# Attention rows scaled by VectorE out of PSUM, and a list schedule that counts the shared SBUF port

## The chip, the core and the metric

The kernel runs on one core of a Trainium2 chip, as one program. Its time is the device time of one execution in microseconds (us). The names of the engines are those of the profile: PE is TensorE's matmul and PEld its weight load, DVE is VectorE, ACT is ScalarE, POOL is GpSimd, SP issues the transfers. PSUM is the memory that PE writes its results to, SBUF the one that the other operands lie in.

## The reference

Three layers follow one another: a causal attention with a decay, and two MLPs. The sizes are batch 4, 8 heads, 576 positions, head size 64; then 2304 tokens of width 512, with hidden widths 1536 and 2048.

```python
def _attn_ref(q, k, v, f):
    scores = scale * np.matmul(q, k.transpose(0, 1, 3, 2))
    cum = np.cumsum(np.log(np.clip(f, 0.0001, 1.0)), axis=-1)
    decay = cum[:, :, :, None] - cum[:, :, None, :]
    scores = np.where(causal, -1000000000.0, scores + decay)
    scores = scores - np.max(scores, axis=-1, keepdims=True)
    attn = np.exp(scores)
    attn = attn / (np.sum(attn, axis=-1, keepdims=True) + 1e-09)
    return np.matmul(attn, v)

def _moe_ref(x, w_a, w_b, w_out):
    return ((x @ w_a) * (x @ w_b)) @ w_out

def _moe2_ref(x, w_in, w_out):
    h = x @ w_in
    g = np.where(h >= 1, h, np.where(h <= -1, 0.0, (h + 1) ** 2 / 4))
    return g @ w_out
```

The attention's result, with the heads side by side, is the first MLP's input, and the MLPs' matmuls are the bulk of the arithmetic.

## The kernel before

Two parts follow one another. The early part holds all the attention and, beside it, the first group of the first MLP for three of the four batches; the late part holds the rest of the MLPs.

**Attention.** Heads go in pairs (`pp`), 16 in all, four to a batch. A head has five chunks of 128 query rows; the fifth has 64 real rows, so the two heads of a pair share one. A pair is seven rounds (`PAIR_ROUNDS`): chunks 0 and 1, then 2, then 3 of the first head, the shared fifth chunk, then the same three of the second head. A round makes scores in a PSUM tile `s` (PE), adds the mask and finds each row's extreme `nm` (DVE, tile `prob`; the order lists this instruction as ISA), takes the exponential (ACT), transposes blocks of `prob` into a PSUM tile `tp` (PE), splits them into two fp16 parts, `th` (ACT) and `tl` (DVE), and multiplies them with the values, also two parts, `vh` and `vl`, into the PSUM tile `o` (PE). The values carry one more column of ones, so column 64 of `o` is the row's sum. The tile `o` has one PSUM bank in all; it is filled 48 times, three times per pair: first head, fifth chunk, second head.

**The scaling of the rows** (end of `pv_step`) is what the change is about. Before, ACT copies `o` into SBUF (`on`, `on4`); DVE makes the divisor `z` from column 64 and `sc`, takes its reciprocal, and the rows are multiplied into `xt`: by GpSimd for a head's four full chunks (128x256), by two DVE instructions (64x64 each) for the fifth chunk.

**Scaling the values.** For each pair, `v_max`, `v_top`, `v_scale` and `v_split` find a power of two per head and split the values. `v_top` ends with `dg`, a 2x2 DVE instruction that PE waits for.

**The order.** In the early part no call issues an instruction at once. An object, `Plan`, records them all and then writes a list schedule: `cost` gives each operation a duration, `forward` steps through time engine by engine and takes, of the operations that are ready, the one of the highest rank, `backward` makes new ranks from the last round's finish times, and after 20 rounds the best order found is issued. Where the model sees PE idle for over `HEAT` = 150 ns, `forward` puts filler matmuls (`mm<-mask`, 128x224, results unused) into PE's queue. Each engine then works through its queue in order, and waits where an operand isn't there. In the trace, all that `Plan` issues has line L279 (L298 after the change); the fillers are L932 (L948). The late part is not recorded by `Plan`; its first matmuls have the lines L512 to L514 (`mm3`).

**Weights.** Blocks of weights come as 64-bit numbers (`wraw`) and are decoded by ACT (`wm`, `wr`), DVE (`wm` clamped, `wt`) and GpSimd (`wt`, `whi`, `wlo`); a few of these blocks are decoded in the early part.

Of the kernel before, what the change touches and what calls it, by code (L numbers as in the profile page):

```python
# [21 lines left out]
P = 128  # L22
# [17 lines left out]
NPB = 3  # L40
LAND = 1030.0
SWITCH = 300.0
HEAT = 150.0
COLD = 6000.0
NEVER = 1.0e18
# [24 lines left out]
class Plan:  # L70
# [5 lines left out]

    def __init__(self, nc):
        self.nc = nc
        self.ops = []
        self.seen = {}  # L80
        self.boost = 0.0
        self.heat = None
# [29 lines left out]
    @staticmethod  # L112
    def cost(engine, method, out, src, args):
        n = max(x.size() // x.shape[0] for x in [out] + (src if engine == "vector" else []))
        if engine == "tensor":
            if method == "transpose":
                return 109.0, 53.0
            size = mybir.dt.size(args["rhs"].dtype)
            passes = 4 if args["rhs"].dtype == F32 else 1
            return passes * max(n / 2.4, 24.0) + 3.0, (107.0 if size == 4 else 27.0)  # L120
        if engine == "vector":
            fast = method in ("tensor_scalar", "tensor_copy", "memset")
            fixed = 66.0 + 61.0 * any(x.shape[-1] == 1 for x in src)
            return fixed + (0.53 if fast else 1.05) * n, 0.0
        if engine == "scalar":
            near = any(x.space == bass.MemoryType.PSUM for x in src)
            return (187.0 if "bias" in args or "scale" in args and not near else 51.0 if near else 90.0) + 0.833 * n, 0.0
        if engine == "gpsimd":
            if method == "tensor_tensor":
                return 55.0 + 2.26 * n, 0.0  # L130
            return 76.0 + 115.0 * any(x.shape[-1] == 1 for x in src) + n, 0.0
        return (650.0 if out.shape[0] == 64 else 475.0), 0.0

    def add(self, engine, method, a, kw):
        names = {"out": a[0]} if a else {}
        names.update(kw)
        out = names["out"]
        writes = [out] + [x for x in (kw.get("accum_out"),) if x is not None]
        reads = [x for x in list(a[1:]) + [x for k, x in kw.items() if k not in ("out", "accum_out")]
                 if isinstance(x, bass.AP)]  # L140
        if method == "tensor_tensor_reduce":
            writes.append(reads.pop())
        me, need = len(self.ops), set()
        for ap, wr in [(x, False) for x in reads] + [(x, True) for x in writes]:
            if ap.space == bass.MemoryType.DRAM:
                if ap.tensor.name not in self.nc_inputs:
                    box = (0, 1, 0, 1, False)
                else:
                    continue
            else:  # L150
                box = Plan.area(ap)
            psum = ap.space == bass.MemoryType.PSUM
            if psum:
                box = (box[0], box[1], 0, 2048, box[4] and box[3] - box[2] == 2048)
            stores, loads = self.seen.setdefault(ap.tensor.name, ([], []))
            need.update(j for old, j, _ in stores if Plan.meet(old, box))
            if wr or psum:
                need.update(j for old, j, other in loads if Plan.meet(old, box) and (wr or other != engine))
            if wr:
                stores[:] = [x for x in stores if not Plan.within(x[0], box)]  # L160
                loads[:] = [x for x in loads if not Plan.within(x[0], box)]
            (stores if wr else loads).append((box, me, engine))
        need.discard(me)
        dur, load = Plan.cost(engine, method, out, reads, names)
        done = dur
        if engine == "sync":
            done = (1275.0 if out.shape[0] == 64 else 625.0, out.size() * mybir.dt.size(out.dtype) / 360.0)
        self.ops.append((engine, method, a, kw, sorted(need), dur, load, done, self.boost))

    def lag(self, j, i):  # L170
        a, b = self.ops[j], self.ops[i]
# [17 lines left out]
    def forward(self, rank):  # L189

        ops, n = self.ops, len(self.ops)
        missing = [len(op[4]) for op in ops]
        ready = [0.0] * n
        wait = {e: [] for e in Plan.ENGINES}
        for i, op in enumerate(ops):
            if not missing[i]:
                wait[op[0]].append(i)
        soon = {e: min((ready[i] for i in wait[e]), default=NEVER) for e in Plan.ENGINES}
        free = {e: 0.0 for e in Plan.ENGINES}
        last = {e: 1e9 for e in Plan.ENGINES}  # L200
        begin, finish, fill = [0.0] * n, [0.0] * n, []
        moved = 0.0
        for _ in range(n):
            t, e = min((max(free[e], soon[e]), e) for e in Plan.ENGINES)
            idle = t - free[e]
            i, best = -1, 0.0
            for j in wait[e]:
                if ready[j] <= t:
                    value = rank[j] - SWITCH * max(0.0, ops[j][6] - last[e] - idle)
                    if i < 0 or value > best or value == best and j < i:  # L210
                        i, best = j, value
            wait[e].remove(i)
            _, _, _, _, _, dur, load, done, _ = ops[i]
            t = max(t, free[e] + load - last[e])
            if e == "sync":
                moved = max(t + done[0], moved) + done[1]
                done = moved + LAND - t
            if e == "tensor" and t - free[e] >= HEAT:
                step = 100.0 if free[e] > COLD else 190.0
                fill += [(free[e] + j * step, n) for j in range(int((t - free[e] - HEAT) // step) + 1)]  # L220
            begin[i], finish[i] = t, t + done
            free[e], last[e] = t + dur, dur
            for j, gap in self.after[i]:
                ready[j] = max(ready[j], t + done + gap)
                missing[j] -= 1
                if not missing[j]:
                    wait[ops[j][0]].append(j)
                    soon[ops[j][0]] = min(soon[ops[j][0]], ready[j])
            soon[e] = min((ready[j] for j in wait[e]), default=NEVER)
        return begin, finish, fill  # L230
# [42 lines left out]
    def issue(self):  # L273
        for i in self.order():
            if i == len(self.ops):
                self.heat()
                continue
            engine, method, a, kw = self.ops[i][:4]
            getattr(getattr(self.nc, engine), method)(*a, **kw)  # L279
        self.ops, self.seen = [], {}  # L280


class Ring:
# [16 lines left out]
def tile_decay_attention__then__moe__then__moe2(  # L300
# [417 lines left out]
    def v_top(pp):  # L718
# [5 lines left out]
        nc.vector.tensor_scalar(m2[:, 0:1], m2[:, 0:1], 2.0 ** -86, None, ALU.max)  # L724
        nc.vector.tensor_scalar(m2i[:, 0:1], m2i[:, 0:1], 0x7F800000, None, ALU.bitwise_and)
        dg = sm_p.tile([2, 2], BF16, name="dg", tag="dg")
        nc.vector.tensor_scalar(dg, ident[0:2, 0:2], m2[:, 0:1], 2.0 ** -14, ALU.mult, ALU.mult)
        vst[pp] = dg

    def v_scale(pp):  # L730
# [101 lines left out]
    def pv_step(k):  # L832
# [5 lines left out]
        if a is not None:  # L838
# [5 lines left out]
            for c in chunks:  # L844
                pv(o[:, c, :], pv_seq(where, c, a, slice(0, P), vv))
            if chunks[-1] == NCH - 2:
                on = sm_p.tile([P, NCH - 1, D + 1], F32, name="on", tag="on", bufs=1)
                nc.scalar.copy(on, o)
                z = sm_p.tile([P, NCH - 1], F32, name="z", tag="z")
                nc.vector.tensor_scalar(z, on[:, :, D], PSC * 1e-9, sc[:, a:a + 1], ALU.add, ALU.mult)  # L850
                nc.vector.reciprocal(z, z)
                nc.gpsimd.tensor_tensor(xt[:, 0:NCH - 1, h * D:(h + 1) * D], on[:, :, 0:D],
                                        z.unsqueeze(2).to_broadcast([P, NCH - 1, D]), ALU.mult)
        else:
            o = ps_o.tile([P, 512], F32, name="o", tag="o")[:, 0:D + 1]
            on = sm_p.tile([P, D + 1], F32, name="on4", tag="on4", bufs=1)
            z = sm_p.tile([P, 1], F32, name="z4", tag="z4")
            halves = [slice(i * TAIL, (i + 1) * TAIL) for i in range(2)]
            seqs = [pv_seq(where, NCH - 1, i, halves[i], vv) for i in range(2)]
            for j in range(len(seqs[0])):  # L860
                for i in range(2):
                    l, r = seqs[i][j]
                    nc.tensor.matmul(o[halves[i], 0:r.shape[1]], lhsT=l, rhs=r, start=j == 0,
                                     stop=j == len(seqs[0]) - 1)
            nc.scalar.copy(on, o)
            for i in range(2):
                rows = slice(i * TAIL, (i + 1) * TAIL)
                nc.vector.tensor_scalar(z[rows], on[rows, D:D + 1], PSC * 1e-9, sc[rows, i:i + 1], ALU.add, ALU.mult)
            nc.vector.reciprocal(z, z)
            for i in range(2):  # L870
                rows = slice(i * TAIL, (i + 1) * TAIL)
                h = (2 * pp + i) % H
                nc.vector.tensor_scalar(xt[rows, NCH - 1, h * D:(h + 1) * D], on[rows, 0:D], z[rows], None, ALU.mult)

    NHH = B * H

# [191 lines left out]
```

## Time and profile before

| | |
|---|---|
| median of 3 runs (least to most) | 1097.97 us (1097.09 to 1098.0) |
| the profiled execution | 1095.04 us |
| its span, first to last instruction | 1093.2 us |
| PE busy | 1060.0 us (97%) |
| DVE busy | 663.5 us (61%) |
| ACT busy | 482.7 us (44%) |
| POOL busy | 605.6 us (55%) |
| last early (L279) instruction on POOL ends | 285.4 us |

The trace is of one execution. Busy is the time in which an engine had at least one instruction running; a DVE instruction's profiled span includes the time for which it is held after it was issued, and it overlaps a little with the next one's. Matmuls are pipelined, so the span of one is longer than the step to the next. The chain of waits goes back from the end of a stretch: at each step to what released the instruction, or to the one before it on its engine. A share of busy time over the whole span mixes the early and the late part, which have different limits, so the rows below are by stretches.

### The profile page before, as it was taken

The numbers are of one execution on the slowest core, as the hardware profiler recorded it, in microseconds if no ns is written. First come the engines' busy times: TensorE is split into PE (matmuls) and PEld (weight loads), VectorE is DVE, ScalarE is ACT, GpSimd is POOL, SyncE is SP. The second block draws the span as 40 slices with busy tenths as digits, with TensorE's granted clock in tenths as the row PEclk, the third lists the DMA queues.
The fourth block names the chain that finished last, engine by engine and source line by source line (L and its number), as shares of the span: only waits on it lengthen the run. The fifth ranks groups of instructions, "written<-read, shape, count | busy, mean of one in ns | idle before, by whom it ended". The sixth has DMA issues, their size and how long they took to land.

```text
span 1093.2 us, 19541 instructions
## 1 busy us (share of the span) xinstructions
PE 1060.0 (97%) x7475; PEld 1000.9 (92%) x7475; DVE 663.5 (61%) x1388; ACT 482.7 (44%) x970; POOL 605.6 (55%) x594
## 2 busy tenths in 40 slices
PE   7898889999899999999999999999999999999998
PEld 5677788998899999999999999999999999999998
DVE  6999989878873462552742833832684487355333
ACT  5788768877541231221321333643552234233221
POOL 7688778665692461641722856932772296156121
PEclk7999989999999999999999999999999999999999
DMA  8444534421230120110210300210220021010111
GB/s 243 144 143 123 164 108 139 128 83 50 62 113 20 38 79 1 59 58 1 77 39 1 98 19 1 78 39 1 78 78 1 1 97 58 1 40 10 57 46 64
DMA packets 22830, 72.12 MB, mean 66 GB/s; under 512 B 2840, under 2 KB 5912, under 8 KB 22736
## 3 DMA queue, kind: packets, MB, share of 16 engines
q1 hardware_dynamic: 22736, 70.87, 21.1%
q8 instruction: 59, 0.97, 0.4%
q14 instruction: 35, 0.29, 0.1%
HBM read 60.26 MB, written 5.96 MB: 61 GB/s over the span
## 4 chain that ended last, share of the span: by engine, by line
PE 76%; DVE 12%; POOL 5%; DMA 3%; issue 2%; ACT 1%; DVEq 0%; SPq 0%; POOLq 0%; ACTq 0%
PE mm L513 21%; PE mm L512 21%; PE mm L514 21%; PE s L279 4%; PE mm L279 4%; PE tp L279 4%; PE o L279 2%; DVE prob L279 2%; DVE tl L279 2%; POOL wlo L479 2%; DMA wraw<-in_w_dram 2%; DVE z L279 1%; POOL wt L466 1%; DVE wt L463 1%; DVE wm L457 1%
## 5 line engine op out<-in xcount | busy, mean ns | idle before, releaser
L513 PE MATMUL mm<-xl,whi 128*128 128x432 f32 (+1 forms) x896 | 299.7, 335 | 1.6 <-DVE xl L926 1.6
L514 PE MATMUL mm<-xh,wlo 128*128 128x432 f32 (+1 forms) x896 | 299.5, 335 | 0.0
L512 PE MATMUL mm<-xh,whi 128*128 128x432 f32 (+1 forms) x896 | 298.8, 335 | 0.1
L513 PE MATMUL mm<-al,whi 128*128 128x432 f32 (+1 forms) x640 | 212.6, 336 | 0.1
L514 PE MATMUL mm<-ah,wlo 128*128 128x432 f32 (+1 forms) x640 | 211.9, 335 | 0.0
L512 PE MATMUL mm<-ah,whi 128*128 128x432 f32 (+1 forms) x640 | 201.9, 336 | 2.2 <-ACT ah L567 2.2
L626 POOL TENSOR_TENSOR al<-tmp,ah 128x432 fp32r<-128x432 f32 (+1 forms) x96 | 103.8, 1082 | 169.2 <-ACT ah L625 169.2
L513 PEld LDWEIGHTS mm<-xl,whi 128*128 128x128 f32 x896 | 168.2, 188 | 5.8 <-DVE xl L926 1.9
L514 PEld LDWEIGHTS mm<-xh,wlo 128*128 128x128 f32 x896 | 168.2, 188 | 3.9
L512 PEld LDWEIGHTS mm<-xh,whi 128*128 128x128 f32 x896 | 167.8, 188 | 4.3 <-DVE tmp L566 0.4
L568 POOL TENSOR_TENSOR al<-tmp,ah 128x432 fp32r<-128x432 f32 (+1 forms) x64 | 67.9, 1062 | 175.4 <-ACT ah L567 175.4
L512 PEld LDWEIGHTS mm<-ah,whi 128*128 128x128 f32 x640 | 118.0, 188 | 6.9 <-ACT ah L567 3.6
L513 PEld LDWEIGHTS mm<-al,whi 128*128 128x128 f32 x640 | 119.9, 188 | 4.6 <-POOL al L568 1.5
L514 PEld LDWEIGHTS mm<-ah,wlo 128*128 128x128 f32 x640 | 119.8, 188 | 3.4
L623 ACT ACTIVATE tmp<-tmp,half 128x432 f32<-128x432 f32 (+1 forms) x96 | 59.1, 616 | 133.3 <-DVE tmp L622 132.9
L566 DVE TENSOR_TENSOR tmp<-mm,tmp 128x432 f32<-128x432 f32 (+1 forms) x64 | 35.0, 548 | 135.1 <-PE mm L514 135.0
L466 POOL TENSOR_TENSOR wt<-wt,wr 128x512 int32<-128x512 int32 x60 | 82.3, 1371 | 15.4 <-DVE wt L463 14.7
L279 ACT ACTIVATE prob<-prob,nm 128x128 f32<-128x128 f32 (+3 forms) x144 | 81.1, 584 | 20.4 <-DVE nm L279 19.3
L479 POOL TENSOR_TENSOR wlo<-wt,whi 128x512 fp32r<-128x512 f32 x62 | 88.4, 1427 | 2.4
L624 DVE TENSOR_TENSOR tmp<-tmp,mm 128x432 f32<-128x432 f32 (+1 forms) x96 | 52.9, 552 | 58.4 <-ACT tmp L623 55.7
L622 DVE TENSOR_SCALAR tmp<-mm 128x432 f32<-128x432 f32 (+1 forms) x96 | 53.2, 554 | 56.6 <-PE mm L514 56.3
L279 PE MATMUL tp<-ident,prob 128*128 128x128 f32 x400 | 78.1, 290 | 6.0 <-DVE m L279 3.5
(127 smaller groups left out, 1999.1 us busy)
## 6 DMA issues: line engine op xcount, KB each, us to landing
wraw<-in_w_dram SPq DMA_DIRECT2D x68, 512.0 KB
raw<-in_qk_dram SPq DMA_DIRECT2D x26, 608.0 KB
vraw<-in_v_dram SPq DMA_DIRECT2D x16, 320.0 KB
qk<-q SPq DMA_DIRECT2D x28, 160.0 KB
out_dram<-tmp SPq DMA_DIRECT2D x16, 216.0 KB
cum_d<-xh SPq DMA_DIRECT2D x1, 1216.0 KB
y<-in_qk_dram SPq DMA_DIRECT2D x2, 608.0 KB
out_dram<-tmp SPq DMA_DIRECT2D x8, 144.0 KB
```

The costliest lines, as they stand in the source:

```text
L279: getattr(getattr(self.nc, engine), method)(*a, **kw)
L466: nc.gpsimd.tensor_tensor(t, t, r, ALU.add)
L479: nc.gpsimd.tensor_tensor(lo, t.rearrange("p (u c) -> p u c", u=UB), V(hi), ALU.subtract)
L512: nc.tensor.matmul(o, lhsT=wh, rhs=xh, start=first, stop=False)
L513: nc.tensor.matmul(o, lhsT=wh, rhs=xl, start=False, stop=False)
L514: nc.tensor.matmul(o, lhsT=wl, rhs=xh, start=False, stop=last)
L566: after(4, lambda: nc.vector.tensor_tensor(pr, ob, asb, ALU.mult))
L568: after(6, lambda: nc.gpsimd.tensor_tensor(al, pr, V(ah), ALU.subtract))
L622: nc.vector.tensor_scalar(t, o, 1.0, -1.0, ALU.min, ALU.max)
L623: after(1, lambda: nc.scalar.activation(t, t, AF.Square, scale=0.5, bias=half))
L624: after(2, lambda: nc.vector.tensor_tensor(r, t, o, ALU.max))
L626: after(4, lambda: nc.gpsimd.tensor_tensor(al, r, V(ah), ALU.subtract))
```

## The change

Two things change. First, the scaling of the rows reads `o` in PSUM: ACT's copies are gone, `z` is made from `o`, and all the products into `xt` are DVE's; `dg` is written by two instructions of one column each. Second, `Plan` knows which operations use the SBUF port that DVE shares with GpSimd (`shares`): in `forward` such an operation starts only after the other engine's last such one has ended, and one that would be held loses rank (`PORT` = 10 per ns). Two durations in `cost` are raised as well. The late part's code is the same.

```diff
             passes = 4 if args["rhs"].dtype == F32 else 1
-            return passes * max(n / 2.4, 24.0) + 3.0, (107.0 if size == 4 else 27.0)
+            return passes * max(n / 2.4, 24.0) + (14.0 if size == 4 else 3.0), (107.0 if size == 4 else 27.0)
...
             if method == "tensor_tensor":
-                return 55.0 + 2.26 * n, 0.0
+                return 95.0 + 2.26 * n, 0.0
...
+    def shares(engine, method, out, src):
+        if engine == "gpsimd":
+            return True
+        if engine != "vector" or out.space == bass.MemoryType.PSUM:
+            return False
+        wide = [x for x in src if x.space != bass.MemoryType.PSUM and x.size() // x.shape[0] > 1]
+        if any(x.space == bass.MemoryType.PSUM for x in src):
+            return False
+        return len(wide) > 1 or len(wide) == 1 and method in ("tensor_scalar", "tensor_copy")
...
+            held = max(0.0, port["vector" if e == "gpsimd" else "gpsimd"] - t)
...
-                    value = rank[j] - SWITCH * max(0.0, ops[j][6] - last[e] - idle)
+                    value = rank[j] - SWITCH * max(0.0, ops[j][6] - last[e] - idle) - PORT * held * self.port[j]
...
+            if self.port[i]:
+                t += held
+                port[e] = t + dur
...
-        nc.vector.tensor_scalar(dg, ident[0:2, 0:2], m2[:, 0:1], 2.0 ** -14, ALU.mult, ALU.mult)
+        for i in range(2):
+            nc.vector.tensor_scalar(dg[:, i:i + 1], ident[0:2, i:i + 1], m2[:, 0:1], 2.0 ** -14, ALU.mult, ALU.mult)
...
-                on = sm_p.tile([P, NCH - 1, D + 1], F32, name="on", tag="on", bufs=1)
-                nc.scalar.copy(on, o)
                 z = sm_p.tile([P, NCH - 1], F32, name="z", tag="z")
-                nc.vector.tensor_scalar(z, on[:, :, D], PSC * 1e-9, sc[:, a:a + 1], ALU.add, ALU.mult)
+                nc.vector.tensor_scalar(z, o[:, :, D], PSC * 1e-9, sc[:, a:a + 1], ALU.add, ALU.mult)
                 nc.vector.reciprocal(z, z)
-                nc.gpsimd.tensor_tensor(xt[:, 0:NCH - 1, h * D:(h + 1) * D], on[:, :, 0:D],
+                nc.vector.tensor_tensor(xt[:, 0:NCH - 1, h * D:(h + 1) * D], o[:, :, 0:D],
                                         z.unsqueeze(2).to_broadcast([P, NCH - 1, D]), ALU.mult)
...
-            nc.scalar.copy(on, o)
...
-                nc.vector.tensor_scalar(z[rows], on[rows, D:D + 1], PSC * 1e-9, sc[rows, i:i + 1], ALU.add, ALU.mult)
+                nc.vector.tensor_scalar(z[rows], o[rows, D:D + 1], PSC * 1e-9, sc[rows, i:i + 1], ALU.add, ALU.mult)
...
-                nc.vector.tensor_scalar(xt[rows, NCH - 1, h * D:(h + 1) * D], on[rows, 0:D], z[rows], None, ALU.mult)
+                nc.vector.tensor_scalar(xt[rows, NCH - 1, h * D:(h + 1) * D], o[rows, 0:D], z[rows], None, ALU.mult)
```

The whole early order is written anew. At DVE, for the last head of the first batch, stood before (`z4` and `on4` are the fifth chunk's, `s` and `tp` are PSUM tiles; the number behind a name is its buffer):

```order
L279 TENSOR_SCALAR xt_128<-on4_0_165,z4_1_173 64x64
L279 ISA prob1_122,nm_3_157<-s_2_152,mask_104 128x320
L279 ISA nm_3_157 128x1
L279 TENSOR_SCALAR z_1_168<-on_0_161,sc_0_142 128x4
L279 SCALAR_TENSOR_TENSOR tl_0_150<-tp_1_141,th_0_149 128x384
L279 RECIPROCAL z_1_168<-z_1_168 128x4
L279 TENSOR_SCALAR xt_128<-on4_0_165,z4_1_173 64x64
L279 SCALAR_TENSOR_TENSOR tl_2_159<-tp_0_138,th_2_158 128x384
```

And on the same engine at the same head stands now:

```order
L298 ISA prob0_121,nm_2_151<-s_1_147,mask_104 128x512
L298 ISA nm_2_151 128x1
L298 TENSOR_SCALAR z_1_166<-o_0_155,sc_0_142 128x4
L298 TENSOR_SCALAR wt_0_169<-wm_0_168 128x512
L298 RECIPROCAL z_1_166<-z_1_166 128x4
L298 SCALAR_TENSOR_TENSOR tl_0_150<-tp_1_141,th_0_149 128x384
L298 TENSOR_TENSOR xt_128<-o_0_155,z_1_166 128x4x64
L298 SCALAR_TENSOR_TENSOR tl_2_159<-tp_0_138,th_2_158 128x384
```

The product into `xt` has come to DVE from GpSimd, two places behind the reciprocal, and `o` is read from the first to the last of these steps; a weight step `wt` and a `tl` stand between them.

On PE, between the second head of the third pair and the first head of the fourth, stood before (`o` is the bank with the results, `tp` the transposes, `s` the scores):

```order
L279 MATMUL o_0_155<-vh0_124,tl_2_159 128x65
L279 MATMUL tp_0_138<-ident_103,prob1_122 128x128 x3
L279 MATMUL s_0_144<-k1_1_116,q1_1_115 128x384
L279 MATMUL tp_1_141<-ident_103,prob2_123 128x128 x3
L279 MATMUL s_0_144<-qk2_1_117 128x384
L279 MATMUL tp_1_141<-ident_103,prob2_123 128x128
L279 LDWEIGHTS th_0_149
L279 MATMUL o_0_155<-vh1_125,th_0_149 128x65
```

And on PE at the same place stands now:

```order
L298 MATMUL o_0_155<-vh0_124,tl_2_159 128x65
L298 MATMUL tp_1_141<-ident_103,prob2_123 128x128 x4
L298 MATMUL s_0_144<-k1_1_116,q1_1_115 128x384
L298 MATMUL s_0_144<-qk2_1_117 128x384
L298 MATMUL s_1_147<-k1_1_116,q1_1_115 128x512
L298 MATMUL s_1_147<-qk2_1_117 128x512
L298 MATMUL tp_2_148<-ident_103,prob0_121 128x128 x3
L298 MATMUL tp_0_138<-ident_103,prob0_121 128x128 x2
L298 MATMUL s_2_152<-k1_0_113,q1_0_112 128x128
L298 MATMUL s_2_152<-qk2_0_114 128x128
L298 LDWEIGHTS th_0_149
L298 MATMUL o_0_155<-vh1_125,th_0_149 128x65
```

Two transposes and four score products more now stand between the last matmul into the bank and the next one. The number of fillers on PE goes from 99 to 160: ahead of the first scores from 64 to 62, behind them from 35 to 98.

## Rows read from the trace of the kernel before

**Rows 1.** Windows: stretch, us, busy us of PE, PEld, DVE, ACT, POOL; clock; DMA.
```profile
40.00:143.00 103.00, 88.60 (x1074) 74.29 (x1075) 100.22 (x304) 80.31 (x179) 83.19 (x83) 0.99 0.47 142
143.00:160.00 17.00, 17.00 (x138) 16.33 (x138) 12.54 (x39) 11.66 (x25) 10.72 (x11) 0.73 0.29 96
160.00:286.00 126.00, 122.08 (x1442) 112.52 (x1441) 104.90 (x340) 98.35 (x227) 82.03 (x88) 1.00 0.32 95
286.00:1093.00 807.00, 799.19 (x4608) 774.08 (x4606) 415.81 (x630) 267.03 (x497) 403.56 (x365) 1.00 0.14 44
```

**Rows 2.** Chain of waits, shares by line, 40 to 143 us.
```profile
by line: DVE prob L279 16.6%; DVE tl L279 15.1%; DVE z L279 9.0%; PE s L279 8.1%; PE tp L279 7.3%; DVE xt L279 6.1%; DVE dg L279 5.9%; DMA vraw<-in_v_dram 5.5%; issue 5.1%; DVE mx L279 4.5%; PE o L279 4.3%; PE mm L279 3.0%; DVE wt L279 2.4%
```

**Rows 3.** DVE groups, 40 to 143 us: busy us, mean ns | idle.
```profile
L279 DVE TENSOR_SCALAR z<-on,sc 128x4 f32<-128x4 f32 x14 | 9.0, 646 | 0.0
L279 DVE TENSOR_SCALAR xt<-on,z 64x64 f32<-64x64 f32 x12 | 7.9, 661 | 0.2
L279 DVE TENSOR_SCALAR dg<-ident,m 2x2 bf16<-2x2 f32 x6 | 6.5, 1085 | 0.0
L279 DVE TENSOR_SCALAR z<-on,sc 64x1 f32<-64x1 f32 x12 | 2.4, 202 | 0.2
```

**Rows 4.** Timeline, 138 to 143 us, DVE, POOL, PE: start, length.
```profile
138.79 1.60 DVE L279 TENSOR_SCALAR z<-on,sc 128x4 f32<-128x4 f32 x1
140.30 0.68 DVE L279 SCALAR_TENSOR_TENSOR wt<-wraw,wt 128x512 int32<-128x512 int32 x1
140.90 1.61 DVE L457 TENSOR_SCALAR wm<-wm 128x512 f32<-128x512 f32 x1
...
138.79 1.57 POOL L279 TENSOR_TENSOR q<-raw,q 64x640 fp32r<-64x640 f32 x1
...
142.86 0.45 PE L279 MATMUL tp<-ident,prob 128*128 128x128 f32 x1 [2.78 <-DVE m L279]
```

**Rows 5.** Tile tmp, late (ns least/median/most); DVE groups, 40 to 143.
```profile
L622 DVE TENSOR_SCALAR tmp<-mm x96: 446/600/610, 687.8 to 1083.0; 128x432 f32<-128x432 f32 x64, 128x288 f32<-128x288 f32 x32
...
L279 DVE CUSTOM_DVE_ANT_0 prob<-s,mask 128x384 f32<-128x384 f32 x13 | 7.0, 542 | 0.2 <-PE tp L279 0.2
L279 DVE CUSTOM_DVE_ANT_0 prob<-s,mask 128x256 f32<-128x256 f32 x13 | 5.3, 408 | 0.0
L279 DVE RECIPROCAL z<-z 128x1 f32<-128x1 f32 x6 | 0.9, 154 | 0.0
L279 DVE RECIPROCAL sc<-tp 128x2 f32<-128x2 f32 x6 | 0.9, 150 | 0.0
```

**Rows 6.** Groups by shape, ACT and POOL, 0 to 286 us.
```profile
L279 ACT COPY on<-o 128x260 f32<-128x260 f32 x32 | 11.9, 373 | 5.2 <-PE o L279 3.4 <-POOL q L279 1.5
...
L279 POOL TENSOR_TENSOR xt<-on,z 128x256 f32<-128x256 f32 x32 | 20.2, 632 | 24.7 <-DVE z L279 17.3 <-ACT prob L279 2.6 <-ACT th L279 1.7
```

**Rows 7.** PE waits, 40 to 143 us: us in total, times, longest.
```profile
PE tp L279 <- DVE m L279: 3.5, 2, 2.8
PE tp L279 <- DVE dg L279: 3.5, 4, 1.4
PE o L279 <- ACT on L279: 0.5, 1, 0.5
```

**Rows 8.** Chain of waits, shares by line, 143 to 286 us.
```profile
by line: PE mm L279 28.8%; PE tp L279 20.4%; PE s L279 17.4%; PE o L279 13.3%; DVE prob L279 4.1%; DVE tl L279 2.7%; issue 1.8%; DVE z L279 1.4%; ACT th L279 1.2%; ACT prob L279 1.1%; POOL wlo L479 0.9%; DVE xt L279 0.8%; DVE dg L279 0.7%; 
```

**Rows 9.** Filler matmuls: timeline, early; group by shape, 40 to 143 us.
```profile
8.90 2.67 PE L932 MATMUL mm<-mask 128*128 128x224 bf16 x26
...
L932 PE MATMUL mm<-mask 128*128 128x224 bf16 x30 | 5.4, 261 | 0.0
```

**Rows 10.** Timeline, PE: one head's last o matmul, next head's first.
```profile
68.29 0.19 PE L279 MATMUL o<-vh,tl 128*128 128x65 f16 x1
...
69.63 0.19 PE L279 MATMUL o<-vh,th 128*128 128x65 f16 x1
```

**Rows 11.** Timeline, PE, the first score matmul.
```profile
14.40 0.38 PE L279 MATMUL s<-y 66*128 66x128 f32 x1 [2.83 <-DMA y<-y]
```

More of the change, by code (lines that the diff above doesn't have):

```diff
@@ L42 @@
 SWITCH = 300.0
+PORT = 10.0
 HEAT = 150.0
@@ L78, in __init__ @@
         self.nc = nc
-        self.ops = []
+        self.ops, self.port = [], []
         self.seen = {}
@@ L129, in cost @@
             if method == "tensor_tensor":
-                return 55.0 + 2.26 * n, 0.0
+                return 95.0 + 2.26 * n, 0.0
             return 76.0 + 115.0 * any(x.shape[-1] == 1 for x in src) + n, 0.0
         return (650.0 if out.shape[0] == 64 else 475.0), 0.0
+    @staticmethod
+    def shares(engine, method, out, src):
[7 more added lines that the diff above has]
+        return len(wide) > 1 or len(wide) == 1 and method in ("tensor_scalar", "tensor_copy")
     def add(self, engine, method, a, kw):
@@ L168, in add @@
         self.ops.append((engine, method, a, kw, sorted(need), dur, load, done, self.boost))
+        self.port.append(Plan.shares(engine, method, out, reads))
     def lag(self, j, i):
@@ L200, in forward @@
         last = {e: 1e9 for e in Plan.ENGINES}
+        port = {"vector": 0.0, "gpsimd": 0.0}
         begin, finish, fill = [0.0] * n, [0.0] * n, []
@@ L279, in issue @@
             getattr(getattr(self.nc, engine), method)(*a, **kw)
-        self.ops, self.seen = [], {}
+        self.ops, self.port, self.seen = [], [], {}
 class Ring:
@@ L855, in pv_step @@
             o = ps_o.tile([P, 512], F32, name="o", tag="o")[:, 0:D + 1]
-            on = sm_p.tile([P, D + 1], F32, name="on4", tag="on4", bufs=1)
             z = sm_p.tile([P, 1], F32, name="z4", tag="z4")
```

## The prediction

> **What bounds the kernel now.** I read the table by stretches first, and the reader should read across each row: in 286 to 1093 us PE is busy 799.19 of 807 us, so the two MLPs are PE's own work; the diff doesn't touch them [rows 1]. All that can move lies before 286 us, in the part whose order the list schedule writes. From 40 to 143 us it is DVE that is full, 100.22 of 103 us, while PE has 14.4 us idle; from 143 us on it is the other way round, PE 17.00 of 17 and 122.08 of 126 us, DVE 104.90 of 126 [rows 1]. So a DVE microsecond saved between 40 and 143 us should count nearly whole, and later hardly.
>
> The chain of waits says the same of that stretch: three small DVE steps, z 9.0%, xt 6.1% and dg 5.9%, are 21.0% of 103 us, 21.6 us; neither ScalarE's copy nor GpSimd's product, which the change removes, is among the lines named [rows 2]. The grouped rows say why these steps are large. A z of 128x4 takes 646 ns on average, a z of 64x1 takes 202 ns, though three more elements can't cost 0.4 us; xt of 64x64 takes 661 ns and dg, four numbers, 1085 ns [rows 3]. The timeline shows what they wait for: a z issued at 138.79 us ends at 140.39, and the GpSimd product issued at 138.79 ends at 140.36; the clamp wm after it is held 1.61 us, and PE stands 2.78 us behind all this [rows 4]. A multi-element DVE instruction from SBUF to SBUF is held until the running GpSimd instruction ends.
>
> **The change part by part.** (1) z, xt and dg out of GpSimd's way, in 40 to 143 us. z and xt now read PSUM, dg becomes two one-element instructions. The one-element z form shows 202 ns [rows 3]. For reading PSUM, the late DVE tensor_scalar out of PSUM ran 96 times between 446 and 610 ns in two sizes, and no instance is long, with GpSimd half busy beside it (403.56 of 807 us) [rows 1, 5]. So I price z at 0.21 us (as the one-element form). xt has 64 elements, bounded by 0.15 us (a two-element reciprocal from PSUM) and 0.41 us (256 elements from PSUM) [rows 5]; I take 0.27, since 64 lies nearer the first. dg is 2 x 0.20. The steps: z 9.0 - 14 x 0.21 = 6.1 us saved, xt 7.9 - 12 x 0.27 = 4.7, dg 6.5 - 12 x 0.20 = 4.1; together 14.9. If PSUM reads were held just the same, only dg's 4.1 would remain; if xt came down to 0.15, 16.3.
>
> (2) The product moves to DVE: 128x256 out of PSUM with z broadcast. The nearest row is the 256-element score pass out of PSUM, 408 ns [rows 5]; 14 of them are 5.7 us added. DVE is 9.2 us lighter in this stretch. Their starts follow more closely than their durations say (the step after the z of 138.79 starts before that z ends, and wm at 140.90, 0.6 us after it), so 14 x 0.33 = 4.6 us is the low end.
>
> (3) ScalarE loses 11.9 us of big copies and GpSimd 20.2 us of products [rows 6]. Neither was named on the chain in 40 to 143 us [rows 2] and ScalarE was busy 80.31 of 103 us [rows 1]; I count the removal itself at nothing. With less GpSimd time there are fewer things to be held by; the clamp wm still reads SBUF and can still be held.
>
> A page of the Trainium skill speaks against moving this work to DVE: Perfetto Trace Analysis, "Optimizing Scalar/DVE Operations", gives a DVE access overhead of about 125 ns on PSUM against about 60 on SBUF, and advises taking work off DVE when it is saturated, which it is here. By that, 65 ns on each z and xt (38 in the stretch) is an estimate of 2.5 us lost again, and the sum below would be 6.2 instead of 8.7. The rows don't show the surcharge: a reciprocal reading PSUM takes 150 ns and one reading SBUF 154 [rows 5]; I leave it out.
>
> (4) 143 to 286 us. z, xt and dg are 1.4, 0.8 and 0.7% of the chain over 143 us, 4.1 us [rows 8]. In the full stretch 14.9 of 23.4 us of such time goes, 64%; the same share here is 2.6 us, and the 18 products added sit on an engine that is not the bound. I take 1.5 us; bounds 0 and 4.1.
>
> (5) At the start the first scores wait 2.83 us for a transfer [rows 11], and a faster dg ahead of them gains nothing: 0, and 2.83 as the most.
>
> (6) The new order. The recorded order has 160 filler matmuls on PE where there were 99: 62 ahead of the first scores (64 before), then 98 in place of 35. One costs 2.67 / 26 = 0.10 us back to back [rows 9]; 61 more are 6.2 us if none falls in an idle moment, and nothing if all do. In 40 to 143 us PE had 14.4 us idle and 30 fillers already [rows 1, 9], so I take 1.0 us.
>
> (7) The one PSUM bank for o is held longer. Before, one ScalarE copy of 0.37 us frees it [rows 6]. Now z, reciprocal and product must all run; in the order shown they stand with one wt and one tl between them. By rows: 0.21 + 0.55 + 0.15 + 0.55 + 0.41 = 1.9 us, some 1.5 us more; the 0.55 is the 542 ns of a score pass over 384 elements [rows 5], for tl, which has as many, and as an estimate for wt. PE meanwhile has more other work in the order: before, seven transposes and two score products between two heads, which took from 68.29 to 69.63 us [rows 10]; after, nine transposes and six score products, so about 2.2 us if the six more cost what the nine did, 0.15 us each. 2.2 against 1.9 leaves 0.3 us of cover for semaphores and a late DVE. Waiting for o cost 0.5 us in that stretch [rows 7]. I take 1.0 us more over all 48 releases; it can be 0 or, without cover, 48 x 1.5.
>
> Sum: -9.2 - 1.5 + 1.0 + 1.0 = -8.7 us. Made against the profiled execution's 1095.04 us (span 1093.2 and 1.84 around it) this is 1086.3; that execution ran 2.93 us under the median of the timed runs, 1097.97, so in their terms the forecast is 1089.3 us.
>
> **What is late next.** Once DVE is lighter, PE. Its idle time leaves 14.4 us open in the stretch, and 5.4 us more are fillers [rows 9], so 9.2 us fit, and twice that wouldn't.
>
> **Rivals.**
> A, more: the 2.78 us stall at 140 us [rows 4] goes entirely and with it the lower clock behind it. From 143 to 160 us the granted clock was 0.73 [rows 1], so 17 x 0.27 / 0.5 = 9.2 us ran at 1.2 GHz and cost 4.6 us. For: z's hold started the chain. Against: wm, in the same queue, was held as long and still can be. With both gone: 8.7 + 2.8 + 4.6 = 16.1, so 1081.9 us.
> B, no change: PE takes over at once. All 61 fillers then lie on its path, 6.2 us in place of 1.0, and waits for o cost 3.5 in place of 1.0: -9.2 - 1.5 + 6.2 + 3.5 = -1.0, 1097.0 us. Against: of PE's waits there, 3.5 us each were for DVE's m and dg, two steps that stand behind held instructions [rows 7].
> C, slower: the o bank. A release waits behind whatever DVE holds, and PE, in order, stands with every transpose and score product behind that matmul. It gives back the whole gain at 9.7 / 48 = 0.20 us per release; at 0.3 us it costs 14.4, so -10.7 + 1.0 + 14.4 = +4.7, 1102.7 us. For: the cover is only some 0.3 us in the order shown, and DVE runs late when full. Against: the order lays more PE work into that gap than before.
> D, it doesn't do what it says: PSUM readers are held too, and the product as well (0.4 us more on each of 14). Then 4.1 us are saved against 5.7 + 5.6 added, 7.2 us worse: 1105.2 us. Against: the 96 even durations [rows 5].
>
> **How the numbers follow.** Forecast 0.55 (1085 to 1094), A 0.20, B 0.11, C 0.12, D 0.02. A measurement of this kernel can't tell less than about 0.2%, 2.2 us, from no change. Forecast and A are faster by more, B is no change, C and D slower: 0.75, 0.11, 0.14. The range 1079 to 1099 leaves out the far part of A (0.05) and most of C and D (0.13); it also holds the two ends of (2) and the fillers at 0 or 6.2 us.
>
> **What would show it.** Right: z of 128x4 near 0.2 us and dg near 0.2 with no instance above 0.3; the product near 0.4 and never above 0.5; DVE's busy time up to the end of the early part lower by more than 9 us; the first instruction of the late part on PE some 8 us sooner; the late part again 807 us long. Wrong: z, xt or the product with instances over 0.6 us (D); PE waiting for DVE's xt before an o matmul for over 10 us in total (C); fillers in a stretch where PE has no idle time (B); a late part of another length, which nothing here foresees.

## The result and the profile after

The changed kernel took 1080.34 us, the median of 4 runs (1077.97 to 1083.1), beside 1097.72 us before (4 runs, 1097.09 to 1098.0): a ratio of 0.9843, 95% interval 0.9817 to 0.9869. On another chip it took 1082.03 us beside 1097.14, ratio 0.9874 (0.9857 to 0.9892). So it gained 17.4 and 15.1 us where 8.7 were forecast. The profiled execution took 1079.24 us, its span is 1077.5 us.

I read the table by stretches first (columns as in [rows 1]; the two first rows lie ahead of those shown of before):

```profile
0.00:14.00 14.00, 8.73 (x67) 7.34 (x68) 7.79 (x20) 7.35 (x10) 8.66 (x33) 1.00 0.86 226
14.00:40.00 26.00, 25.48 (x189) 18.29 (x188) 19.58 (x71) 16.99 (x36) 14.60 (x14) 0.80 0.56 160
40.00:143.00 103.00, 100.30 (x1240) 88.63 (x1238) 100.15 (x354) 86.64 (x180) 86.23 (x82) 1.00 0.54 163
143.00:160.00 17.00, 15.51 (x191) 13.99 (x190) 16.11 (x54) 13.16 (x29) 12.25 (x12) 1.00 0.53 166
160.00:268.00 108.00, 105.14 (x1252) 98.21 (x1250) 87.70 (x310) 79.45 (x174) 61.05 (x60) 1.00 0.30 86
268.00:1077.00 809.00, 800.87 (x4609) 775.79 (x4607) 413.44 (x631) 267.35 (x498) 402.97 (x365) 1.00 0.14 44
```

From 40 to 143 us PE was busy 88.60 us before [rows 1] and is now busy 100.30, with 90 fillers in it where there were 30; DVE is as full as before, with 354 instructions in place of 304. From 143 to 160 us the clock was 0.73 and is 1.00. The early part ends some 18 us sooner, and the late part is a little longer.

The steps themselves, by tile (ns least/median/most, first and last start):

```profile
L298 DVE TENSOR_SCALAR z<-o,sc x64: 184/216/226, 27.7 to 264.8; 128x4 f32<-128x4 f32 x32, 64x1 f32<-64x1 f32 x32
...
L298 DVE TENSOR_TENSOR xt<-o,z x32: 392/414/425, 30.1 to 265.2; 128x256 f32<-128x256 f32 x32
L298 DVE TENSOR_SCALAR xt<-o,z x32: 266/283/293, 34.6 to 261.9; 64x64 f32<-64x64 f32 x32
...
L298 DVE TENSOR_SCALAR dg<-ident,m x32: 174/195/204, 8.2 to 246.3; 2x1 bf16<-2x1 f32 x32
```

None is held any more: the longest z takes 226 ns, where the mean of 128x4 was 646 [rows 3]. The weight steps that still read SBUF are held as before (`wm` of DVE, 818 ns and 849 before; mean in the stretch from 40 to 143 us, with the product's and the fillers' groups there; columns as in [rows 3]):

```profile
L298 DVE TENSOR_SCALAR wm<-wm 128x512 f32<-128x512 f32 x5 | 4.1, 818 | 0.0
L298 DVE TENSOR_TENSOR xt<-o,z 128x256 f32<-128x256 f32 x14 | 5.7, 410 | 0.0
...
L948 PE MATMUL mm<-mask 128*128 128x224 bf16 x90 | 13.4, 261 | 0.5 <-ACT tmp L298 0.5
```

The chain in the same stretch, by line, and then all of PE's waits there (us in total, times, longest):

```profile
by line: PE s L298 15.4%; PE tp L298 15.3%; PE o L298 12.1%; DVE tl L298 11.0%; DVE prob L298 10.6%; PE mm L298 7.3%; PE mm L948 5.8%; DVE xt L298 3.3%; issue 3.1%; DVE xl L298 2.8%; DVE z L298 2.8%; DVE wt L298 2.7%; DVE mx L298 1.5%; DVE 
```
```profile
PE o L298 <- DVE m L298: 0.8, 1, 0.8
PE o L298 <- DVE xt L298: 0.6, 2, 0.3
PE mm L948 <- ACT tmp L298: 0.5, 1, 0.5
PE tp L298 <- ACT prob L298: 0.4, 1, 0.4
```

z, xt and dg were 21.0% of this chain [rows 2]; z and xt are 6.1% of it now, and dg is no longer among the lines named. PE's own lines lead, and the fillers (L948) are 5.8% of it.

Where the microseconds lie is read from the end of each pair, that is of its last matmul into `o`, in the two profiled executions:

| stretch | before, us | after, us | difference |
|---|---|---|---|
| start to end of pair 1 | 41.6 | 36.5 | -5.1 |
| pairs 2 to 7 | 87.4 | 83.0 | -4.4 |
| pair 8 | 20.4 | 14.1 | -6.3 |
| pairs 9 to 16 | 132.7 | 131.1 | -1.6 |
| from there to the first late matmul | 2.5 | 1.6 | -0.9 |
| late part | 808.6 | 811.2 | +2.6 |

The two orders lay other work into a pair, so the rows of pairs 2 to 7 and of pair 8 are safest read together: 107.8 us before, 97.1 after.

### The profile page after: what moved, and what is told of

Read it like the earlier page. It is cut to its first block, busy times and chain, and to the rows that moved or that the text cites. A ratio compares the mean times of both kernels' runs of the same rounds, so it can differ in the third digit from the quotient of the medians.

```text
span 1077.5 us, 19591 instructions
## 1 busy us (share of the span) xinstructions
PE 1056.0 (98%) x7536; PEld 1002.3 (93%) x7536; DVE 644.8 (60%) x1436; ACT 471.0 (44%) x922; POOL 585.8 (54%) x562
## 4 chain that ended last, share of the span: by engine, by line
PE 81%; DVE 7%; POOL 5%; DMA 3%; issue 2%; ACT 1%; SPq 0%; DVEq 0%; POOLq 0%; ACTq 0%
PE mm L532 21%; PE mm L531 21%; PE mm L533 21%; PE s L298 5%; PE mm L298 4%; PE tp L298 4%; PE o L298 3%; POOL wlo L498 2%; DMA wraw<-in_w_dram 2%; POOL wt L485 1%; DVE tl L298 1%; DVE prob L298 1%; POOL whi L497 1%; POOL al L587 1%; DVE wt L482 1%
## 5 line engine op out<-in xcount | busy, mean ns | idle before, releaser
L584 ACT COPY tmp<-mm 128x432 f32<-128x432 f32 (+1 forms) x64 | 30.1, 471 | 110.7 <-PE mm L533 110.7
```

## The experiments

Beside each time stands its ratio to the kernel before, run beside it on the same chip, with the 95% interval. In nearly every profile TensorE's clock is 1.2 GHz for a stretch near the start, mostly from 13 to 18 us on. It was 10.2 to 37.5 us long from one profile to the next, 3.4 us in one and missing in one. So a time also depends on that: single executions of the kernel before lay between 1089.74 and 1100.53 us. Profiles are set side by side by the length of that stretch, and single executions by their mean granted clock, though a kernel's own idle time can lower that too.

**The scaling alone.** The new scaling and the two dg instructions, with the old costs and no port rule:

```diff
+        return False          # first line of shares()
-            ... + (14.0 if size == 4 else 3.0), ...
+            ... + 3.0, ...
-                return 95.0 + 2.26 * n, 0.0
+                return 55.0 + 2.26 * n, 0.0
```

> The scaling out of PSUM and the split dg, with the list schedule's old costs and without its rule on the port. Theory H (what counts is that z, xt and dg are no longer held by GpSimd): most of the 17.4 us stay, 1080 to 1085 us; z near 0.21, xt 0.28, dg 0.20, product 0.41 us, as after. Theory O (what counts is the new order, which knows the port): 5 us at most, 1092 us or more, though the same durations are seen.

1084.82 us, 0.9885 (0.9862 to 0.9909). Its runs fall into two groups, 1081.3 to 1082.4 at a mean clock of 0.990 to 0.992 and 1087.2 to 1088.3 at 0.981 to 0.983. Most of the gain is here; the first group lies where the changed kernel lies at that clock (1080.7 to 1082.62 at 0.990 to 0.992, in the run called after again).

**The planner alone.** The new costs and the port rule, with the scaling of before:

> The list schedule with the port rule and the new costs, on the old scaling (copy by ScalarE, product by GpSimd, 2x2 dg). Theory H: 1094 to 1100 us, since an order can move the held instructions but not the time for which GpSimd runs; z of 128x4 still has instances over 0.6 us. Theory O: 1084 to 1090 us, z and dg now stand where GpSimd is free, their means fall to under 0.4 us.

1095.06 us, 0.9987 (0.9973 to 1.0): almost nothing. Its dg and z (columns as in [rows 3], over the whole early part) and PE's wait for `m`:

```profile
L298 DVE TENSOR_SCALAR z<-on,sc 128x4 f32<-128x4 f32 x32 | 16.2, 506 | 2.5 <-ACT on L298 2.5
L298 DVE TENSOR_SCALAR dg<-ident,m 2x2 bf16<-2x2 f32 x16 | 4.9, 304 | 0.1
```
```profile
PE tp L298 <- DVE m L298: 1.1, 1, 1.1
```

z is still held. dg's mean did fall, as theory O had it, from 783 ns to 304, by its place in the order. And the stall at 140 us [rows 4] is gone: PE is busy 12.98 of the 13 us from 130 to 143, and the clock is 1.00 from there to 160 us. Yet pairs 2 to 8 take 107.3 us, as before (pair 8 10.8, pairs 2 to 7 96.5).

**The port rule off**, new costs kept (`return False` in `shares`, the rest as after):

> The changed kernel with its new costs but without the port rule in the list schedule. Theory H: within 2 us of the changed kernel, 1078 to 1082 us, because few held instructions are left for the rule to place. Theory O: 1088 us or more.

1085.33 us, 0.9896 (0.9869 to 0.9923). This lies between the two ranges. At equal clock (0.992: 1080.83 and 1081.97) it is no slower than the changed kernel's 1077.97 to 1083.1 by more than its own scatter.

**dg alone.** The order of before, frozen; each 2x2 dg is issued as two instructions of one column:

```diff
+            if engine == "vector" and method == "tensor_scalar" and tuple(a[0].shape) == (2, 2):
+                for c in range(2):
+                    self.nc.vector.tensor_scalar(a[0][:, c:c + 1], a[1][:, c:c + 1], *a[2:], **kw)
+                continue
```

> The kernel before, its order kept word for word, but each dg issued as two one-element instructions. Theory H: dg falls from 0.78 to 0.20 us each, 6 us of DVE time, and PE's 6.0 us of waits for dg mostly go: 1092 to 1095 us. Rival: DVE's next hold (z, xt or wm) takes its place, and the lower clock at 143 us stays: 1096 to 1098 us.

1089.58 us, 0.9943 (0.9923 to 0.9964): some 6 us for two small instructions in place of one, more than either range had. The tile rows for dg, of before and of this run, and the wait that stays (views as above):

```profile
L279 DVE TENSOR_SCALAR dg<-ident,m x16: 190/765/1573, 8.5 to 264.3; 2x2 bf16<-2x2 f32 x16
L281 DVE TENSOR_SCALAR dg<-ident,m x32: 173/195/203, 9.6 to 259.9; 2x1 bf16<-2x1 f32 x32
```
```profile
PE tp L283 <- DVE m L283: 3.6, 2, 2.8
```

The 2.8 us stall at 140 us [rows 4] and a low clock behind it are still there, so these 6 us lie elsewhere: pairs 2 to 7 take 82.8 us in place of 87.4.

**After again**, the changed kernel on the chip of the next three:

> The changed kernel once more, beside the others of this set, since a kernel's runs differ with the time that PE spends at the lower clock. 1078 to 1083 us, granted clock 0.990 to 0.993; if long stretches at 1.2 GHz at the start (30 us, as in the profiles of the scaling alone and of the port rule left out) come here too, single runs of 1085 us and more.

1082.03 us, 0.9874 (0.9857 to 0.9892).

**The low clock behind the stall.** The kernel before, every instruction in its place, with 26 fillers put where PE stood still at 140 us:

> The kernel before, its order kept, with 26 filler matmuls more in PE's queue just where PE stood idle for 2.78 us at 140 us. If the lower clock behind that idle time cost what rival A said: clock 1.00 from 143 to 160 us and 4 to 5 us less, 1091 to 1092 us. If DVE sets the pace there anyhow: clock up, but under 1.5 us gained. If the fillers only delay PE: no change or slower.

1094.48 us, 0.9979 (0.9965 to 0.9993). The windows around the place, before and then in this run (columns as in [rows 1]):

```profile
140.00:143.00 3.00, 0.22 (x2) 0.17 (x2) 3.00 (x5) 0.93 (x3) 2.16 (x2) 0.80 0.34 73
143.00:150.00 7.00, 7.00 (x52) 6.38 (x53) 6.37 (x21) 4.06 (x10) 4.58 (x5) 0.50 0.29 91
150.00:160.00 10.00, 10.00 (x88) 9.95 (x87) 6.17 (x19) 7.60 (x16) 6.14 (x6) 0.90 0.30 99
```
```profile
140.00:143.00 3.00, 2.16 (x28) 1.65 (x27) 2.97 (x7) 0.63 (x2) 1.29 (x2) 1.00 0.73 262
143.00:150.00 7.00, 6.82 (x87) 6.07 (x87) 7.00 (x13) 5.26 (x13) 5.72 (x5) 1.00 0.18 40
150.00:160.00 10.00, 9.62 (x97) 8.91 (x95) 9.65 (x37) 7.23 (x17) 7.51 (x8) 1.00 0.46 139
```

Before, PE works 0.22 of 3 us and the clock falls to 0.50 behind that; here it works 2.16 and the clock stays at 1.00. Pairs 8 and 9 took 17.6 and 22.0 us in place of 20.4 and 23.0. So the low clock alone costs 2.3 us by the times (0.8 to 3.8 by the interval), 3.8 by the trace; the first range, 4 to 5, was too high.

**No fillers.** The changed kernel, same order, without the 98 fillers behind the first scores:

```diff
+        done = 0
...
             if i == len(self.ops):
-                self.heat()
+                if done <= 2:
+                    self.heat()
                 continue
+            done += self.ops[i][0] == "tensor"
```

> The changed kernel with the same order, but without the 98 fillers behind the first score product (the 62 ahead of it stay). If fillers cost PE time, 1075 to 1079 us. If they are free, as term (6) nearly had it, and nothing else: within 2 us, 1078 to 1082 us. If they hold the clock up: more time at 1.2 GHz, granted clock under 0.985, and 1083 to 1090 us.

1078.10 us, 0.9835 (0.9816 to 0.9855), 4 us under the changed kernel on the same chip (0.9874), though on its first chip the changed kernel had 0.9843.

**From SBUF.** The changed kernel with ScalarE's copies back, and z, xt and the product on DVE from those copies:

```diff
+                nc.scalar.copy(on, o)
...
-                nc.vector.tensor_tensor(xt[:, 0:NCH - 1, h * D:(h + 1) * D], o[:, :, 0:D],
+                nc.vector.tensor_tensor(xt[:, 0:NCH - 1, h * D:(h + 1) * D], on[:, :, 0:D],
...
```

> The changed kernel, product on DVE and dg split, but with ScalarE's copies kept: z, both xt and the product read SBUF, and the list schedule plans them as users of the port. Theory H: they are held again; z and xt over 0.4 us on average, the product of two SBUF operands over 0.6, and the time is 1090 to 1100 us. Theory G (what counts is that GpSimd has less to do, and its product no longer ends the chain): 1079 to 1085 us.

1099.89 us, 1.0034 (1.001 to 1.0058). By tile, the same instructions as after but for the place they read, then their means (columns as in [rows 3], over the whole early part):

```profile
L298 DVE TENSOR_TENSOR xt<-on,z x32: 401/424/1578, 41.1 to 288.8; 128x256 f32<-128x256 f32 x32
L298 DVE TENSOR_SCALAR xt<-on,z x32: 217/254/1434, 50.7 to 286.3; 64x64 f32<-64x64 f32 x32
```
```profile
L298 DVE TENSOR_TENSOR xt<-on,z 128x256 f32<-128x256 f32 x32 | 19.2, 601 | 0.2
L298 DVE TENSOR_SCALAR z<-on,sc 128x4 f32<-128x4 f32 x32 | 17.6, 549 | 0.9 <-ACT on L298 0.8
L298 DVE TENSOR_SCALAR xt<-on,z 64x64 f32<-64x64 f32 x32 | 13.0, 407 | 0.5
```

The medians of the two in the first rows are within 0.03 us of those of after; what differs is the longest, 1578 for 425 ns and 1434 for 293. All three means are above the limits that theory H set, and the three groups keep DVE busy for 49.8 us where the changed kernel's take 29.0 (13.2, 6.8 and 9.0), 20.8 more. The whole gain is gone, though GpSimd is as much relieved as in the changed kernel.

**The product back on GpSimd**, from a copy of ScalarE's; z and the fifth chunk still from PSUM:

> The changed kernel with one part undone: for a head's four full chunks ScalarE copies o again and GpSimd makes the product from the copy; z still reads PSUM, the fifth chunk and dg are as after. If DVE's time is what counts, as term (2) had it (13 us of products more on DVE over the early part): 3 to 6 us faster than the changed kernel, 1075 to 1079 us. If GpSimd's 20 us come back as holds of wm and wt and as a later end of the scaling: 1083 to 1090 us. In any case z stays near 0.21 us.

1081.61 us, 0.9872 (0.9844 to 0.9899): as the changed kernel, and in neither range.

**Two banks for o**, one bank less for the scores:

```diff
-    ps_s = Ring(pool("ps_s", 1, early, space=bass.MemoryType.PSUM), 3)
-    ps_o = Ring(pool("ps_o", 1, early, space=bass.MemoryType.PSUM), 1)
+    ps_s = Ring(pool("ps_s", 1, early, space=bass.MemoryType.PSUM), 2)
+    ps_o = Ring(pool("ps_o", 1, early, space=bass.MemoryType.PSUM), 2)
```

> The changed kernel with two PSUM banks for o in place of one, and two for the scores in place of three. If the longer hold of o costs more than the 1.0 us of term (7): faster than the changed kernel by 2 us or more, 1076 to 1080 us. If it costs nothing, the missing score bank shows: 1082 to 1092 us.

1088.32 us, 0.994 (0.9913 to 0.9967): slower than the changed kernel. A second `o` bank gives less than the exchange costs. That the loss is the missing score bank isn't shown: eight of its ten executions ran at a clock of 0.979 to 0.988, and the one at 0.991 took 1082.17 us, as the changed kernel.

**More fillers ahead of the first scores**, none behind them:

> The changed kernel without the fillers behind the first score product, and with 12 and 30 more ahead of it, where PE waits some 2.7 us for the first transfer. If the lower clock from 15 us on comes from that idle time: no stretch at 1.2 GHz near the start, first pair done by 33 us, 1072 to 1076 us, granted clock over 0.996, and less spread between runs. If it comes from the work of the first scores itself: 1077 to 1080 us as without the fillers.

1078.20 us, 0.9845 (0.9817 to 0.9872): as without fillers. In its profile the clock from 14 to 40 us was 0.93 and the first pair was done at 34.2 us, but the timed runs gained nothing by it.

The kernels so far differ in their number of fillers (62 to 263 in all), and so four of them were run without those behind the first scores.

> The kernel before with its 35 filler matmuls behind the first scores taken out and every other instruction in its place. Theory (fillers cost about 0.04 us each: the changed kernel without its 98 ran 4 us sooner): 1.4 us less than before, 1095 to 1096.5, ratio about 0.9987. Rival (the fillers keep the clock up in this kernel, which has more idle moments): more time at 1.2 GHz, over 1099.

The kernel before without its 35: 1094.4 us, 1.0004 (0.9984 to 1.0024). No difference, so neither theory nor rival; its profile shows two more short stretches at 1.2 GHz, 3.4 us each at 72.6 and 93.1 us.

> The new schedule with the old scaling (the planner alone) without its some 200 fillers behind the first scores. Theory (the port rule is worth little without the scaling; its fillers lie in idle moments): 1091 to 1094, ratio about 0.995 to 0.997. Rival (the order gains some 8 us and its 200 fillers hide it, at 0.04 us each): 1085 to 1088, ratio about 0.991.

The planner alone: 1095.58 us, 1.0007 (0.9983 to 1.0031). Nothing, with fillers or without, less even than the theory's 3 to 5 us.

> The changed kernel with ScalarE's copies kept and z, xt and the product on DVE from SBUF, without its some 200 fillers behind the first scores. Theory (reading PSUM is what gains): still 1093 to 1098, ratio 0.995 to 1.0, some 15 us over the changed kernel without fillers (1078.1). Rival (its fillers were the loss): 1084 to 1088, ratio about 0.99.

From SBUF: 1104.73 us, 1.0087 (1.0062 to 1.0113). Its fillers were not the loss; without them it is slower than the theory had it, at a clock of 0.976 to 0.984.

> The new scaling with the old schedule costs and no port rule, without its some 60 fillers behind the first scores; to be set beside the changed kernel without fillers, 1078.1 us, ratio 0.9835. Theory (the new order adds little): 1078 to 1081, ratio 0.983 to 0.986. Rival (the port rule is worth some 5 us beyond the fillers): 1083 to 1086, ratio about 0.988.

The scaling alone: 1083.06 us, 0.9884 (0.9846 to 0.9921). The changed kernel without fillers stood at 0.9835 (0.9816 to 0.9855). By the medians the new order beside the new scaling is thus worth 0.0049 of 1096, 5 us, as the rival had it. But the intervals overlap, and at equal clock no difference is seen: 1076.85 us at 0.992 and 1074.84 at 0.995 here, 1080.08 and 1075.29 in the changed kernel without fillers.

**Three times the fillers** behind the first scores in the changed kernel:

> The changed kernel with each of the 98 filler matmuls behind the first scores issued three times (196 more), those ahead of them as they are. Theory (a filler costs about 0.04 us, as the run without them said): some 8 us over the changed kernel, 1088 to 1091, ratio 0.993 to 0.995. Rival (they cost nothing, and the 4 us were the clock at the start): 1078 to 1083, ratio 0.985 to 0.988. If each lay wholly on PE's path at 0.10 us it would be 1102.

1093.68 us, 0.998 (0.9961 to 0.9999). 196 more cost 1093.68 - 1082.03 = 11.7 us, 0.06 us each, and most of the gain; that is more than the theory's 8.

## Why the prediction was right in kind and wrong in size

The mechanism stands. z, xt and dg were held, and reading PSUM, or one element from SBUF, ends that: dg alone gives some 6 us with every other instruction in its place, and z, xt and the product from SBUF lose the whole gain (1099.89 and, without fillers, 1104.73 us). The Trainium skill's SBUF — State Buffer, "Who interferes with whom", says that a VectorE instruction with at most one SBUF input, outside the modes that use two ports, doesn't contend with GpSimd. The traces agree: no z, xt or product out of PSUM took over 425 ns. The GpSimd step that held z at 138.79 us is the scaling of `q` [rows 4] and not the product into `xt`; the change leaves that step on GpSimd, and by the tile rows no z out of PSUM is held by it.

The forecast of 8.7 us was about half of what came. The profiled executions differ by 15.7 us, 7.0 more than the sum. The start, which term (5) put at nothing, gave 5.1: that is the step that failed most. Pairs 2 to 8 gave 10.7 where -9.2 + 1.0 + 1.0 makes 7.2; the low clock behind the stall, which the sum left out, is of about the size of that difference (2.3 to 3.8 us), though that it makes it isn't shown. What lies behind pair 8 gave 2.5 where term (4) had 1.5, and the late part took 2.6 back. A part of the gain is the clock (the stretch near the start and the one behind the stall): at a mean clock of 0.992 the two kernels took 1092.02 us and 1080.7 to 1081.44 on the second chip, some 11 us apart where the medians are 15.1 apart. Step by step:

**(1) and (2), the durations: right.** In 40 to 143 us z of 128x4 takes 208 ns (taken: 210), xt 280 (270), dg 195 each (200), the product 410 (408). For the counts of before that is 23.4 - 14 x 0.208 - 12 x 0.280 - 12 x 0.195 = 14.8 us saved, 14.9 forecast. The surcharge for PSUM that the Trainium skill's Perfetto Trace Analysis gives in "Optimizing Scalar/DVE Operations" is smaller here than the 65 ns that I worked out from it: the one-element z takes 214 ns from PSUM and took 203 from SBUF (means over the early part), and the fifth chunk's xt takes 283 ns against a median of 254 from SBUF, 0.03 us more. The product's 5.7 us, though, was charged in full, and with the product on GpSimd the kernel is neither faster nor slower (1081.61 us). Why it costs nothing isn't shown; PE was as good as full.

**(5), the start at nothing: failed.** Pair 1 ends 5.1 us sooner. Part of that is chance, since the low clock at the start lasted 10.2 us in this profile and 13.7 in that of before. At equal length it still is 3 to 4 us: 41.6 us before and 38.1 without fillers at 13.7 us; 42.8 with dg alone and 39.0 in the second run of after at 17.1 us. I had priced only the wait for the transfer [rows 11], 2.83 us and now 2.65, and left out the same held steps of pair 1 (they stand ahead of 40 us, where my stretch began). DVE's timeline of before shows them, 1.7 us longer together than the same steps after (0.22 and 0.29 us):

```profile
31.93 1.08 DVE L279 TENSOR_SCALAR z<-on,sc 128x4 f32<-128x4 f32 x1
33.33 1.15 DVE L279 TENSOR_SCALAR dg<-ident,m 2x2 bf16<-2x2 f32 x1
```

PE's wait there, of before and after (view as above):

```profile
PE tp L279 <- DVE dg L279: 2.1, 2, 1.5
```
```profile
PE tp L298 <- DVE dg L298: 0.8, 1, 0.8
```

How much of the 3 to 4 us these holds make is not shown. At 17.1 us of low clock before would end pair 1 at some 43.3 us (an estimate: 41.6 and half of the 3.4 us more); dg alone ends it at 42.8 and the planner alone at 41.8. So neither gives the whole, and the rest is z and xt out of PSUM or the order made for them.

**Rival A, at 0.20, came, but its reason is shown only in part.** The 2.78 us stall [rows 4] and the low clock behind it are gone, and pair 8 is 6.3 us shorter. My argument against it was that `wm`, in the same queue, was held as long and still can be. The timeline of after, at the same `m` (the ninth pair's; start, length), shows that a weight step is indeed still held there:

```profile
125.69 0.41 DVE L298 TENSOR_TENSOR xt<-o,z 128x256 f32<-128x256 f32 x1
126.02 1.80 DVE L298 TENSOR_SCALAR wt<-wm 128x512 int32<-128x512 int32 x1
127.74 0.27 DVE L298 TENSOR_REDUCE m<-tp 2x1 f32<-2x128 f32 x1
```
```profile
128.40 0.23 PE L298 MATMUL o<-vh,tl 128*64 128x65 f16 x2 [0.76 <-DVE m L298]
```

A `wt` of 1.80 us stands directly ahead of `m`, and PE waits 0.76 us for `m`. Before, three steps of 1.60, 0.68 and 1.61 us stood there [rows 4], and PE waited 2.78. So here PE's queued work covers most of one held step, and there it did not cover two held steps with a third between them; I had asked only whether a hold remains, not how much of it PE can cover. With dg alone mended, in the old order, the stall stays at 2.8 us. But the planner alone also does away with the stall, with z still held (506 ns on average), and gains nothing. So the new order suffices for that, and that z's relief would have done it in the old order isn't shown. The lower clock was put too high, 4.6 us for the 2.3 to 3.8 measured. That the sum of A, 8.7 + 2.8 + 4.6 = 16.1, lies by the result is luck in part: it has nothing for the start, and nothing for the late part.

**(4): right, with luck.** -1.5 was forecast, and -1.6 came in pairs 9 to 16. But without fillers these pairs take 129.0 us and not 131.1, so a larger gain and a cost that (6) had too small offset each other.

**(6), the fillers: mis-sized.** The 63 more behind the first scores cost 0.04 us each by the run without them and 0.06 by the run with three times as many, 2.5 to 3.8 us where I took 1.0. The first of the two is less sure, since the changed kernel's 0.9843 on its first chip would make it 0.01. In the profile without them pairs 2 to 7 take 81.4 us in place of 83.0: they lay on PE's path there, with PE busy 100.30 of 103 us.

**(7), the bank of `o`: 0.6 us** of PE's waits for xt, 1.0 taken, and rival C with it gone. B falls by the result, D by the tile rows.

**The late part: not foreseen**, 2.6 us longer. The windows of after show where:

```profile
274.00:278.00 4.00, 1.41 (x9) 0.96 (x8) 3.90 (x7) 2.23 (x6) 3.83 (x4) 1.00 0.42 135
278.00:282.00 4.00, 4.00 (x21) 4.00 (x20) 3.26 (x4) 2.56 (x6) 4.00 (x4) 0.57 0.36 131
282.00:286.00 4.00, 4.00 (x33) 4.00 (x32) 1.88 (x3) 1.61 (x4) 4.00 (x5) 1.00 0.39 131
```

PE is idle for 2.6 us at the seam of the two parts (1.6 us for DVE's `xl`, as before, and 1.0 for ScalarE's `xh`, which is new), and then has 3.4 us at 1.2 GHz. Half of these lost (an estimate) and the 1.0 make 2.7.

**Open**: what the new order is worth beside the new scaling (5 us by the medians, nothing at equal clock), what part of it the raised costs have, and why the planner alone gains nothing though dg's holds and the stall at 140 us go. The old order with z and xt read from PSUM wasn't tried.

## What to carry to other kernels

A tiny VectorE instruction with a long mean duration was being held here; look for what runs on GpSimd in that time, and try reading PSUM or single elements before moving work between engines. Price such a step over the whole stretch in which it occurs, the start too, and look in the new order at what now stands ahead of the instruction that TensorE waited for. Once TensorE is full, fillers that cost nothing before can be a cost: leave them out and measure, as the changed kernel without them has the lowest median here (1078.10 us).

## What the runs showed of the hardware

- TensorE's clock was at 1.2 GHz after the start for 10.2 us in one execution of the changed kernel and 17.1 us in another, 30.7 us with the scaling alone and not at all near the start in an execution of the same kernel without fillers behind the first scores (1074.84 us, the shortest of all; there it fell at 68.5 us, for 6.8). What sets it was not found; with more fillers ahead of the first scores it was 3.4 us in the profile, and the median gained nothing.
- The clock fell behind stalls of 2.6 and 2.78 us, for 3.4 and 10.2 us, and without fillers it fell in places where it had not: 3.4 us each at 72.6 and 93.1 us in the kernel before. The time did not change by it (1.0004).
- A 2x2 VectorE instruction from SBUF took 190 to 1573 ns (16 of them), and a 2x1 never over 203 (32 between 173 and 203 ns): with every other instruction in its place that was worth 6 us (0.9943).
- The same 2x2 took 304 ns on average in an order that knows the port, and no gain was seen with it (0.9987); why is open.
